# Attention with cluster routing, then a gated feed-forward layer: one more head loaded in half rows, and four pieces of work put elsewhere in the queues

## The chip, the cores and the metric

The kernel runs on one core of a Trainium2 chip. The metric is the device time of one execution in microseconds (us); the kernel before takes 328.75 us in the median of six runs (328.22 to 329.19). A trace of one execution shows for every engine what it ran and when. The engines are named as in the profile: PE (TensorE, matrix products), PEld (its weight loads), DVE (VectorE), ACT (ScalarE), POOL (GpSimd) and SP (SyncE, which here only issues transfers). Times such as "at 79.19" are microseconds from the start of the profiled span.

## What is computed

```python
# q, k, v: (4 batches, 8 heads, 768 tokens, 64); centroids: (8 heads, 16 clusters, 64)
q_assign = argmax(normalised q @ normalised centroids.T)      # one of 16 clusters for each query
k_assign = argmax(normalised k @ normalised centroids.T)      # and for each key
scores = where(q_assign == k_assign, q @ k.T / 8, -1e9)       # (768, 768) for each head
x = softmax(scores) @ v, the heads laid side by side          # (3072, 512)
xn = x / rms(x) * rms_g
out = (silu(xn @ w_gate) * (xn @ w_val)) @ w_out              # 512 -> 1536 -> 512, float32
```

The kernel does without a mask. It adds 16 rows to the 64 rows of each head's transposed q and k: a one-hot code of the cluster, scaled. Where two clusters agree, their product adds a constant to the score, which the exponential takes off again.

## The kernel before

**Names and layout.** The 32 (batch, head) pairs are numbered n = 0 to 31, here called heads. Four heads make a group g (8 groups; groups 2 and 3, heads 8 to 15, are the second batch). Half a batch's queries are a unit u (8 units; u = 2 and 3 are the two halves of batch 1, which is made of groups 2 and 3). A unit is 24 steps, three for each of 8 heads, each with two score products (`s`) and an exponential on ACT (`pT`), followed a head later by the product with v (`acc`).

**How a head gets ready.** Its q and k come from memory into `staged` by SP (`load`). Up to head BH - 1 they are loaded whole, one transfer each for q and k (line 88), then transposed on PE into a PSUM tile `tq` (line 221, three products each for q and for k) and copied to `qkT` by ACT (line 227). From head BH on, each of q and k is loaded in four transfers that put 32-element half rows on different partitions (line 96, eight transfers a head), so that DVE can do the whole transposition in blocks of 32 by 32 (line 217) and neither PE nor ACT has a part in it. POOL casts `qkT` to bfloat16 in `qext` and `kext` (line 240); below BH two of the key casts are DVE's. The cluster steps of a group (`cluster_steps`) are: `products` (PE, line 254, tile `sc`, then a DVE transposition), `most`, `same` and `back` (DVE, lines 262, 266, 286), once for queries and once for keys; `place` then copies the codes below the heads by small transfers that POOL issues (line 297). POOL also casts v (`vcast`, line 243) and issues the weight loads, which convert to bfloat16 on the way; `load_o` (line 207) brings a third of the output weights `wo`.

**The feed-forward part.** When a unit's attention is done, `rms` makes `xn` on DVE (line 403) and SP issues a transposing transfer to `xnT` (line 406). Products `gate` and `val` (line 444) follow, 24 per unit, then 9 pieces of output products `o` (line 469). `gate`, `val`, `o`, `tq` and `sc` take turns on three PSUM tiles (`gen`); ACT and DVE turn `gate` and `val` into `gvT` (lines 452, 453 and 457).

**What sets the order.** The order is written out by hand; every engine and every queue runs its part of it in order. While unit u's attention runs, a list `fill` is worked off between the steps: the last 8 `gate`/`val` products of unit u - 2, `rms` of unit u - 1, late loads, the output products of unit u - 2 with the first rows of preparation for group u + 2 between them (`spread`), and 16 `gate`/`val` products of unit u - 1 with the rest of the preparation. In unit 1 the preparation is that of groups 2 and 3 at once: `prep` is the casts `c`, the cluster steps `a`, and a weave of group 3's transpositions `t3` and casts `c3`. A head's loads for later heads are issued in the middle of its own preparation (`others`: v of head n + 4, q and k of head n + 6), except for the heads in `LATE`, which are issued right behind `rms`, and so behind the transposing transfer on SP's queue.

```python
            if n < BH:      # whole rows: PE transposes later
                (on or nc.sync).dma_start(out=staged[n][:, part], in_=src((q, k)[part], n))
            for e in range(2):      # half rows: four transfers for q, four for k
                for c in range(2):
                    nc.sync.dma_start(out=to[r:r + 32], in_=of[e, c])
```

Of the kernel before, what the change touches and what calls it, by code (L numbers as in the profile page):

```python
# [22 lines left out]
def kernel(  # L23
# [12 lines left out]
    nc = tc.nc  # L36
    B, H, S, D = q.shape
# [7 lines left out]
    HG = 4  # L45
# [4 lines left out]
    FC = DF // P  # L50
# [3 lines left out]
    CUT = 2 * FC - 8  # L54
    LEAD = 6
    NQ, NV = 6, 8
    AV = 4
    LATE = [19] + [n for n in range(20, B * H) if n % HG < 2]
    BH = 14
    BG = BH // HG  # L60

    ctx.enter_context(tc.manual_schedule())
# [17 lines left out]
    def src(a, n):  # L80
        b, h = divmod(n, H)
        return a[b, h].rearrange("(p t) d -> p t d", t=ST)

    def load(n, part, on=None):
        if n not in staged:
            staged[n] = stage.tile([P, 2, ST, D], F32, tag="qk", name="qk")
        if n < BH:
            (on or nc.sync).dma_start(out=staged[n][:, part], in_=src((q, k)[part], n))
            return

        to = staged[n][:, part].rearrange("p t d -> p (t d)").rearrange("p (i r d) -> p i r d", i=HT, d=32)
        of = (q, k)[part][n // H, n % H].rearrange("(r p i e) (c d) -> e c p i r d", p=32, i=HT, e=2, d=32)
        for e in range(2):
            for c in range(2):
                r = 32 * (2 * e + c)
                nc.sync.dma_start(out=to[r:r + 32], in_=of[e, c])

    def load_qk(n):
        if n < B * H:
            load(n, 0)  # L100
            load(n, 1)

    def load_v(n, vq=None):
        if n >= B * H:
            return
        stagedv[n] = stage.tile([P, ST, D], F32, tag="vs", name="vs", bufs=NV)
        (vq or nc.sync).dma_start(out=stagedv[n], in_=src(v, n))
# [98 lines left out]
    def load_o(c):  # L206
        nc.gpsimd.dma_start(out=wo[:, c:c + 4], in_=moe_w_out[c * P:(c + 4) * P].rearrange("(c p) f -> p c f", p=P))
# [4 lines left out]
    def trans(g, h, part, on=None):  # L212
        if (g, h // 2) not in qkT:
            qkT[g, h // 2] = qk32.tile([P, 2, 2, UQ], F32, tag="qkT", name="qkT")
        qk = staged[g * HG + h]
        if g * HG + h >= BH:
            nc.vector.transpose(qkT[g, h // 2][:, h % 2, part], qk[:, part].rearrange("p t d -> p (t d)"))  # L217
            return
        ps = ps_g.tile([P, UQ], F32, tag="gen", name="tq")
        for i in range(HT):  # L220
            nc.tensor.transpose(ps[:, i * P:(i + 1) * P], qk[:, part, 2 * i:2 * i + 2].rearrange("p t d -> p (t d)"),  # L221
                                ident_f)
        to, by = qkT[g, h // 2][:, h % 2, part], 1.0 / ZS if part and g < BG else 1.0
        if on is nc.vector:
            nc.vector.tensor_scalar_mul(to, ps, by)  # L225
        else:
            nc.scalar.activation(to, ps, ACT.Copy, scale=by)
# [5 lines left out]
    def cast(on, g, h, part, es=(0, 1)):  # L233
        for e in es:
            to = cols((kext if part else qext)[g % 4][:D, h], g, e)
            of = qkT[g, h // 2][e * D:(e + 1) * D, h % 2, part]
            if on is nc.scalar:
                nc.scalar.copy(to, of)
            else:
                on.tensor_copy(to, of)  # L240

    def vcast(n):
        nc.gpsimd.tensor_copy(vbf[n // HG % 4][:, n % HG, :, :D], stagedv[n])
# [24 lines left out]
    def cluster_steps(g, m):  # L268

        of = {}  # L270

        def products():
            of["cl"] = cluster_products(g, [(h, m) for h in range(HG)])

        def most():
            of["mx"] = largest(of["cl"])

        def same():
            of["ohT"] = asg.tile([P, UQ], BF16, tag="ohT", name="ohT", bufs=2)
            compare(of["ohT"].rearrange("p (b e c) -> p b e c", e=2, c=NC), of["cl"], of["mx"])  # L280

        def back():
            put[g, m] = asg.tile([P, UQ], BF16, tag="oh", name="oh", bufs=3)
            if m and g >= BG:
                nc.vector.tensor_scalar_mul(of["ohT"], of["ohT"], ZS)
            nc.vector.transpose(put[g, m], of["ohT"])  # L286

        return [products, most, same, back]
# [3 lines left out]
    def place(on, g, m, es=(0, 1)):  # L292

        ext = (kext if m else qext)[g % 4]
        for h in range(HG):
            for e in es:
                on.dma_start(out=ext[D:D + NC, h, e * UQ:(e + 1) * UQ],  # L297
                             in_=put[g, m][32 * h + e * NC:32 * h + (e + 1) * NC])
# [190 lines left out]
    def group_work(g):  # L489

        t, c = [], []
        for h in range(HG):
            n = g * HG + h
            w = 0.0 if n >= BH else 0.3
            t += [(w, lambda h=h: trans(g, h, 0)), (w, lambda h=h: trans(g, h, 1))]

            def others(n=n):
                vcast(n)
                load_v(n + AV)
                if n + NQ not in LATE:  # L500
                    load_qk(n + NQ)

            def both(h=h, f=others):
                cast(nc.gpsimd, g, h, 0)
                f()
                cast(nc.gpsimd if g * HG + h >= BH else nc.vector, g, h, 1, (0,))
            if g == 2:
                c.append((0.0, others))
            else:
                c += [(0.0, both), (0.0, lambda h=h: cast(nc.gpsimd if g * HG + h >= BH else nc.vector, g, h, 1, (1,)))]  # L510
        a = []
        for m in range(2):
            a += [(0.0 if i else 0.7, f) for i, f in enumerate(cluster_steps(g, m))]
            if g == 3:
                a.append((0.0, lambda m=m: place(nc.gpsimd, g, m)))
            elif g == 2:
                a.append((0.0, (lambda: (place(nc.gpsimd, g, 1), place(nc.gpsimd, g, 0, (1,)))) if m else
                          (lambda: place(nc.gpsimd, g, 0, (0,)))))
        if g > 3:
            a[:1] = [(1.4, lambda f=(a[0][1], a.pop(4)[1]): [x() for x in f])]  # L520
            a.append((0.0, lambda: [place(nc.gpsimd, g, m) for m in range(2)]))
        return t, c, a

    def weave(t, c):

        return [x for pair in zip(t, c) for x in pair] + c[len(t):]
# [8 lines left out]
    def spread(a, b):  # L535

        if not a:
            return list(b)
        w, n = [], 0
        for i, x in enumerate(a):  # L540
            w.append(x)
            while n < len(b) * (i + 1) // len(a):
                w.append(b[n])
                n += 1
        return w
# [134 lines left out]
    for u in range(1, NU):  # L680
        ffn, o, g = ffn_work(u - 1), out_work(u - 2) if u > 1 else [], u + 2
        if u == 1:
            t, c, a = group_work(2)
            t3, c3, a3 = group_work(3)
            n = LEAD - 4
            o3 = [(0.0, lambda i=i: load_o(i)) for i in range(0, FC, 4)]
            prep = c + a + spread(weave(t3[n:], c3), o3) + a3[:5]
            idle = const.tile([P, 1], BF16)

            def norm():  # L690
                rms(0)
                nc.gpsimd.tensor_copy(idle, xn[0][:, CC - 1, HT - 1, P - 1:])
                for h in range(HG):
                    casts(pool_, H + h, K0, Q0, K1, Q1)

            hooks = {(1, 0, 0): late[6], (1, 0, 1): lambda: (late[7](), norm())}
            hooks.update({(1, *divmod(2 + i, HT)): t3[i][1] for i in range(n)})
            hooks[1, *divmod(LEAD - 1, HT)] = lambda: xtrans_all(0)
            fill = spread(ffn[:CUT], prep)
            attention([(1, h) for h in range(H)], fill, LEAD, hooks)  # L700
        else:
            fill = ffn_work(u - 2)[CUT:]
            if u == 2:
                fill = fill[:1] + spread(fill[1:], [(0.0, f) for _, f in a3[5:]])
            fill.append((0.0, lambda u=u: rms(u - 1)))
            rows, clusters = group(g)
            fill += [(0.0, lambda n=n: load_qk(n)) for n in LATE if n - n % HG == (u + 3) * HG or (u, n) == (2, 19)]
            n = 12 if u == 2 else len(rows)
            fill += spread(o, rows[:n]) + spread(ffn[:CUT], [(0.0, f) for _, f in rows[n:]] + clusters)
            attention([(u, h) for h in range(H)], fill, 1 if g < NG else 0, ahead=1)  # L710
    rest = ffn_work(NU - 2)[CUT:]
    rest[0][1]()
# [39 lines left out]
```

## Time and profile before

| | |
|---|---|
| median of 6 runs | 328.75 us (328.22 to 329.19) |
| the profiled execution, and its span | 328.22 us, 326.4 us |
| busy: PE, DVE, ACT, POOL | 319.3, 222.4, 246.1, 137.5 us |
| one score product, one gate product, in the table of groups | 327 ns, 325 ns |
| one DVE transposition of half a head, line 217 | 549 ns |
| one ACT copy of half a head, line 227 | 497 ns |
| one cast on POOL, line 240 | 541 to 557 ns |
| granted PE clock | 1.00 in each stretch asked for |

The busy time of an engine is the time in which it had an instruction. Products on PE overlap: each of the products above has a busy time of some 325 ns, but a set of four starts 0.65 us ahead of what follows it. What an instruction costs on a full PE is therefore read from one start to the next. A row in a timeline gives start, duration of the merged run, engine, line, operation, what it writes and reads, and how many. SP's rows are issues of transfers: their duration is the time for which the queue was held, and not the transfer itself.

### The profile page before, as it was taken

Reading aid. Unit: us, or ns where it says so; the run is one execution under the profiler, and the core shown is the slowest. Engines: PE = TensorE matmul, PEld = TensorE weight load, DVE = VectorE, ACT = ScalarE, POOL = GpSimd, SP = SyncE. Lnnn points to the kernel's source line nnn. Section 1 sums busy time; section 2 is a strip of 40 time slices with the busy share of each in tenths; the row PEclk is TensorE's granted clock in tenths of the full one; section 3 lists DMA queues with packets and bytes.
Section 4 is the critical chain, followed back from the end, with each engine's and each line's share of the span. In section 5 each row is a group of like instructions: output and inputs, shape, how many; then the busy total and the mean of one; then the engine's idle time right before and its main releaser. Section 6 shows DMA issues by size and latency. Waiting matters only on the chain.

```text
span 326.4 us, 7794 instructions
## 1 busy us (share of the span) xinstructions
PE 319.3 (98%) x2851; PEld 192.0 (59%) x2865; DVE 222.4 (68%) x509; ACT 246.1 (75%) x425; POOL 137.5 (42%) x277
## 2 busy tenths in 40 slices
PE   8999899999999999999999999999999999999996
PEld 4546656655556655665566555665566656655654
DVE  5999978879478676878677785876265645685430
ACT  5899988977769867897778867897779868862322
POOL 6999499995926265441916256350000000000000
PEclk9999999999999999999999999999999999999999
DMA  7999995798546654561545540000700041002002
GB/s 274 373 259 209 230 166 101 126 193 167 95 65 145 142 114 74 120 157 52 100 87 120 154 112 34 8 20 1 148 2 0 2 112 34 0 2 79 20 1 96
DMA packets 88742, 34.24 MB, mean 105 GB/s; under 512 B 70400, under 2 KB 85632, under 8 KB 88704
## 3 DMA queue, kind: packets, MB, share of 16 engines
q1 hardware_dynamic: 79536, 27.45, 35.5%
q0 software_dynamic: 8880, 5.91, 11.1%
q8 instruction: 22, 0.36, 0.5%
q10 hardware_dynamic: 288, 0.39, 0.3%
q14 instruction: 16, 0.13, 0.1%
HBM read 28.61 MB, written 6.29 MB: 107 GB/s over the span
## 4 chain that ended last, share of the span: by engine, by line
PE 87%; DVE 9%; ACT 2%; issue 1%; POOL 0%; DVEq 0%; ACTq 0%; POOLq 0%
PE gate L444 18%; PE val L444 18%; PE o L469 18%; PE s L348 17%; PE acc L366 9%; PE sc L254 3%; ACT pT L352 1%; DVE kext L332 1%; DVE qext L332 1%; PE warm L132 1%; DVE pads L327 1%; PE tq L221 1%; PE o L480 1%; DVE qkT L225 1%; DVE xn L391 1%
## 5 line engine op out<-in xcount | busy, mean ns | idle before, releaser
L352 ACT ACTIVATE pT<-s,off 128x768 bf16<-128x768 f32 x192 | 170.9, 904 | 30.9 <-PE s L348 30.2
L348 PE MATMUL s<-qext,kext 80*128 80x384 bf16 x384 | 94.8, 327 | 1.6 <-ACT pT L352 0.8
L444 PE MATMUL gate<-xnT,wg 128*128 128x384 bf16 x384 | 78.3, 325 | 0.1
L444 PE MATMUL val<-xnT,wv 128*128 128x384 bf16 x384 | 78.1, 326 | 0.0
L453 DVE SCALAR_TENSOR_TENSOR th<-th,gate 128x384 f32<-128x384 f32 x84 | 46.3, 551 | 34.8 <-ACT th L452 34.2
L469 PE MATMUL o<-wo,gvT 128*128 128x512 bf16 x262 | 66.3, 378 | 0.8
L348 PEld LDWEIGHTS <-kext 80*128 80x128 bf16 x384 | 36.4, 98 | 35.1 <-issue 7.5
L452 ACT ACTIVATE th<-gate 128x384 f32<-128x384 f32 x84 | 41.2, 490 | 15.3 <-PE gate L444 14.5
L457 DVE SCALAR_TENSOR_TENSOR gvT<-th,val 128x384 bf16<-128x384 f32 x84 | 46.2, 550 | 9.3 <-PE val L444 3.4
L444 PEld LDWEIGHTS <-wg 128*128 128x128 bf16 x384 | 36.1, 97 | 23.4 <-issue 0.8
L366 PEld LDWEIGHTS <-pT 128*128 128x128 bf16 x1152 | 43.4, 97 | 10.1 <-DVE x L373 1.0
L444 PEld LDWEIGHTS <-wv 128*128 128x128 bf16 x384 | 35.6, 97 | 22.5 <-issue 0.6
L240 POOL CAST qext<-qkT 64x384 bf16<-64x384 f32 x64 | 35.3, 557 | 30.7 <-DVE inv L371 18.4
L366 PE MATMUL acc<-vbf,pT 128*128 128x65 bf16 x1152 | 45.7, 193 | 0.6 <-ACT pT L352 0.2
L469 PEld LDWEIGHTS <-gvT 128*128 128x128 bf16 x276 | 25.9, 97 | 25.6
L297 POOL DMA_DIRECT2D qext<-oh x48 | 23.0, 490 | 32.7 <-DVE oh L286 29.2
L240 POOL CAST kext<-qkT 64x384 bf16<-64x384 f32 x58 | 31.4, 541 | 4.3 <-DVE qkT L225 2.4
L297 POOL DMA_DIRECT2D kext<-oh x48 | 23.1, 488 | 7.5 <-DVE oh L286 7.1
L472 ACT COPY o_sb<-o 128x512 f32<-128x512 f32 x23 | 13.5, 585 | 16.0 <-PE o L469 16.0
L371 DVE RECIPROCAL inv<-acc 128x6 f32<-128x6 f32 x32 | 6.0, 188 | 23.8 <-PE acc L366 23.4
L373 DVE TENSOR_TENSOR x<-acc,inv 128x384 f32<-128x384 f32 x32 | 17.8, 558 | 1.1
L217 DVE STREAM_TRANSPOSE qkT<-qk 128x384 f32<-128x384 f32 x36 | 18.1, 549 | 0.0
(83 smaller groups left out, 230.1 us busy)
## 6 DMA issues: line engine op xcount, KB each, us to landing
vs<-in_v_dram SPq DMA_DIRECT2D x32, 192.0 KB, 4.2
out_dram<-o_sb SPq DMA_DIRECT2D x23, 256.0 KB, 2.7
qk<-in_q_dram SPq DMA_DIRECT2D x72, 48.0 KB, 2.8
qk<-in_k_dram SPq DMA_DIRECT2D x72, 48.0 KB, 2.6
qk<-in_q_dram SPq DMA_DIRECT2D x14, 192.0 KB, 4.1
qk<-in_k_dram SPq DMA_DIRECT2D x12, 192.0 KB, 4.2
wg<-in_moe_w_gate_dram POOLq DMA_DIRECT2D x4, 384.0 KB, 8.5
wv<-in_moe_w_val_dram POOLq DMA_DIRECT2D x4, 384.0 KB, 9.7
```

Source lines behind the costliest of these rows:

```text
L217: nc.vector.transpose(qkT[g, h // 2][:, h % 2, part], qk[:, part].rearrange("p t d -> p (t d)"))
L240: on.tensor_copy(to, of)
L297: on.dma_start(out=ext[D:D + NC, h, e * UQ:(e + 1) * UQ], in_=put[g, m][32 * h + e * NC:32 * h + (e + 1) * NC])
L348: nc.tensor.matmul(ps[:, j, :w] if nt == HT else flat[:, j * w:(j + 1) * w], lhsT=cols(kext[g % 4][:KR, hh], g, kc // HT, kc % HT * P, (kc ...
L352: nc.scalar.activation(pT[u, h][:, n * i:n * i + n, :w], of, ACT.Exp, bias=off, scale=scale if g >= BG else scale * ZS)
L366: nc.tensor.matmul(acc[:, h % 2, t], lhsT=pT[u, h][:, kc, t * P:(t + 1) * P], rhs=vbf[g % 4][:, hh, kc % HT * 2 + kc // HT], start=kc == 0 ...
L373: nc.vector.tensor_tensor(dst, acc[:, :, :nt, :D], inv[:, :, :nt].unsqueeze(3).broadcast_to([P, 2, nt, D]), op=ALU.mult)
L444: nc.tensor.matmul(ps, lhsT=w[:, c, f * P:(f + 1) * P], rhs=xnT[u][:, c, :n], start=c == 0, stop=c == CC - 1)
L452: nc.scalar.activation(th, ps, ACT.Tanh, scale=0.5)
L453: nc.vector.scalar_tensor_tensor(th, th, 1.0, ps, op0=ALU.add, op1=ALU.mult)
L457: nc.vector.scalar_tensor_tensor(gvT[u][:, f, :n], gates[u], 0.5, ps, op0=ALU.mult, op1=ALU.mult)
L469: nc.tensor.matmul(outs[u], lhsT=gvT[u][:, f, t * P:(t + 1) * P], rhs=wo[:, f], start=f == 0, stop=f == FC - 1)
```

## The change

- BH goes from 14 to 13: head 13 is loaded in half rows and transposed on DVE.
- `LATE` becomes a table by unit. Head 18's q and k are no longer loaded from the middle of head 12's preparation in unit 1, but with 19, 20 and 21 behind unit 2's `rms(1)`; heads 24, 25, 28 and 29 stay where they were.
- The first two `load_o` go from the weave of group 3 into group 2's cluster steps, between the placing of the key codes and that of the second half of the query codes. The third goes into the weave behind its fourth entry.
- In unit 2, 8 and no longer 12 of group 4's 16 rows go between the output products; the other 8 (heads 18 and 19) and the first four cluster steps go among the 16 `gate`/`val` products. The key's `most`, `same` and `back`, and the placing, go to unit 3, among its first `gate`/`val` products.

```diff
-    LATE = [19] + [n for n in range(20, B * H) if n % HG < 2]
-    BH = 14
+    LATE = {2: (18, 19, 20, 21), 3: (24, 25), 4: (28, 29)}
+    BH = 13
...
-                if n + NQ not in LATE:
+                if not any(n + NQ in x for x in LATE.values()):
                     load_qk(n + NQ)
...
             elif g == 2:
-                a.append((0.0, (lambda: (place(nc.gpsimd, g, 1), place(nc.gpsimd, g, 0, (1,)))) if m else
-                          (lambda: place(nc.gpsimd, g, 0, (0,)))))
+                a += [(0.0, lambda: place(nc.gpsimd, g, 1)), (0.0, lambda: load_o(0)), (0.0, lambda: load_o(4)),
+                      (0.0, lambda: place(nc.gpsimd, g, 0, (1,)))] if m else [(0.0, lambda: place(nc.gpsimd, g, 0, (0,)))]
...
-            o3 = [(0.0, lambda i=i: load_o(i)) for i in range(0, FC, 4)]
-            prep = c + a + spread(weave(t3[n:], c3), o3) + a3[:5]
+            w3 = weave(t3[n:], c3)
+            prep = c + a + w3[:4] + [(0.0, lambda: load_o(8))] + w3[4:] + a3[:5]
...
-            if u == 2:
-                fill = fill[:1] + spread(fill[1:], [(0.0, f) for _, f in a3[5:]])
+            if u in (2, 3):
+                fill = fill[:1] + spread(fill[1:], [(0.0, f) for _, f in (a3[5:] if u == 2 else rest)])
             fill.append((0.0, lambda u=u: rms(u - 1)))
             rows, clusters = group(g)
-            fill += [(0.0, lambda n=n: load_qk(n)) for n in LATE if n - n % HG == (u + 3) * HG or (u, n) == (2, 19)]
-            n = 12 if u == 2 else len(rows)
-            fill += spread(o, rows[:n]) + spread(ffn[:CUT], [(0.0, f) for _, f in rows[n:]] + clusters)
+            fill += [(0.0, lambda n=n: load_qk(n)) for n in LATE.get(u, ())]
+            n, m = (8, 4) if u == 2 else (len(rows), len(clusters))
+            fill += spread(o, rows[:n]) + spread(ffn[:CUT], [(0.0, f) for _, f in rows[n:]] + clusters[:m])
+            rest = clusters[m:]
```

## The prediction

> **What bounds the kernel now.** I read the page's busy times and its chain first, then PE's timeline around head 13, then SP's queue across units 1 to 3, and the stretches of four microseconds last.
>
> ```profile
> PE 319.3 (98%) x2851; PEld 192.0 (59%) x2865; DVE 222.4 (68%) x509; ACT 246.1 (75%) x425; POOL 137.5 (42%) x277
> PE 87%; DVE 9%; ACT 2%; issue 1%; POOL 0%; DVEq 0%; ACTq 0%; POOLq 0%
> ```
>
> PE is hardly ever without work from 41 us on, and the chain that ended last runs along it. So a microsecond taken from PE's list is a microsecond of the kernel, unless another queue then makes PE wait. Here is head 13, which the change takes off PE:
>
> ```profile
> 51.81 0.51 PE L348 MATMUL s<-qext,kext 80*128 80x384 bf16 x2
> 52.15 0.49 PE L221 MATMUL tq<-ident_f,qk 128*128 128x128 f32 x3
> 52.48 0.81 PE L444 MATMUL val<-xnT,wv 128*128 128x384 bf16 x4
> 53.13 0.51 PE L348 MATMUL s<-qext,kext 80*128 80x384 bf16 x2
> 53.72 0.55 PE L221 MATMUL tq<-ident_f,qk 128*128 128x128 f32 x3
> 54.10 0.81 PE L444 MATMUL gate<-xnT,wg 128*128 128x384 bf16 x4
> 53.72 0.31 PEld L221 LDWEIGHTS tq<-ident_f,qk 128*128 128x128 f32 x3 [0.49 <-ACT qkT L227]
> ```
>
> The reader is to see starts, not durations: the first `tq` pushes its follower from 52.15 to 52.48, the second costs 0.38 and had a hole in front of it, because its PSUM tile came free late. SP's queue is the second thing that has no room:
>
> ```profile
> 71.94 1.81 SPq L107 DMA_DIRECT2D vs<-in_v_dram  x3
> 79.19 1.63 SPq L406 DMA_TRANSPOSE xnT<-xn  x1
> 80.87 2.95 SPq L96 DMA_DIRECT2D qk<-in_q_dram  x4
> 83.87 2.63 SPq L96 DMA_DIRECT2D qk<-in_k_dram  x4
> ...
> 109.45 2.63 SPq L96 DMA_DIRECT2D qk<-in_k_dram  x4
> 112.18 0.56 SPq L473 DMA_DIRECT2D out_dram<-o_sb  x1
> 112.84 0.86 SPq L107 DMA_DIRECT2D vs<-in_v_dram  x2
> 116.45 1.49 SPq L406 DMA_TRANSPOSE xnT<-xn  x1
> ```
>
> From 80.87 to 113.70 SP issues without a pause: five heads in half rows (19 to 23), outputs and v. Then it waits 2.75 us, until `xn` of unit 2 is ready. The transposing transfer at 116.45 took 3.8 us to land, so `xnT` is there at 120.25. Its first reader on PE starts at 123.09:
>
> ```profile
> 122.55 0.71 PE L366 MATMUL acc<-vbf,pT 128*128 128x65 bf16 x18
> 123.09 0.81 PE L444 MATMUL gate<-xnT,wg 128*128 128x384 bf16 x4
> ```
>
> **The change, part by part.**
>
> *Head 13 off PE and ACT.* Two sets of three transpositions. First set: 52.48 - 52.15 = 0.33. Second: the `s` before it needs 0.33 from 53.13, so PE was free at 53.46; `gate` started at 54.10; 0.64 with the hole. Together 0.97 us. The lower end is without the hole, 0.33 + 0.38 = 0.71, if some other tile is late there instead. The hole goes with its cause, though: the tile that the second `tq` takes is the one of `gate` at 51.16, whose DVE reader ran from 53.15 to 53.67; without the two `tq` the third tile back is always one whose reader has been done for 0.9 us or more, by the same timeline. I take 0.97. Here a rule is weighed: the Trainium skill, "TensorE: Matmul & The Clock Gate", section "PE-mode transpose", measures about 275 ns for one 128x128 transposition inside a kernel; six would be 1.65 us (an estimate from that page, for another type). The busy times of the trace (0.49 for three that start 0.11 apart) show why that is too much: they overlap their neighbours. The spacing decides, 0.97. ACT loses two copies of 0.49, which lie beside PE.
>
> *Head 13 on DVE and POOL.* DVE gains two transpositions at 0.55 and gives two key casts at 0.39 to POOL: net +0.3 us between 52 and 62 us. DVE idled there for 0.46 + 0.35 us, and again 0.76 ahead of 63.25, and its work for head 13 begins at 54.24, as before. Laying the new order on these starts, `gvT` follows its `val` by 2.0 to 2.2 us where it was 1.8 to 2.1, and three PSUM tiles leave 0.9 us. Cost nothing; were that cover gone, PE would pay the 0.3. POOL gains two casts, 1.0 us, while group 3's codes are placed at 81.4 and wanted near 93.
>
> *Head 13's loads.* Two whole transfers held SP for 0.80 us (28.75 to 29.55); eight in half rows hold it 5.3 us where nothing else is on (2.63 for four), and 10.6 us (32.80 to 43.43, head 14) in the crowded stretch. Queued behind them are v of heads 8 to 12, then heads 14 and 15. The stretch is full until 46 us and half empty behind (last two figures of a row: share of the transfer engines' time, summed over packets so that it can pass 1, and GB/s):
>
> ```profile
> 40.00:44.00 4.00, 3.73 (x41) 2.30 (x41) 2.46 (x7) 3.50 (x6) 3.20 (x8) 1.00 1.54 213
> 48.00:52.00 4.00, 4.00 (x44) 2.10 (x42) 3.10 (x7) 3.08 (x4) 3.90 (x10) 1.00 0.50 79
> 57.24 0.56 DVE L217 STREAM_TRANSPOSE qkT<-qk 128x384 f32<-128x384 f32 x1
> 60.82 0.57 DVE L217 STREAM_TRANSPOSE qkT<-qk 128x384 f32<-128x384 f32 x1
> ```
>
> Everything behind is 4 to 6 us later. Heads 14 and 15 (the last two lines: their key transpositions) then land at 52 to 54 and 56 to 59 in place of 47.6 and 53; they are wanted at about 57 and 60. v of 8 to 11 lands by 46 and POOL takes it at 49.16. Nothing waits if the delay stays under 6 us. I cost it at zero; at 8 us PE would pay about 1.5.
>
> *Head 18 behind the transposing transfer.* Unit 1's queue loses 7.6 us (64.30 to 71.94) and is early again, but the transfer at 79.19 waited for `xn`, not for SP: no gain. In unit 2 the queue gains eight issues. What was head 19's slot (80.87) now holds 18; DVE wants 18 where it wanted 19 (88.44), and that one didn't wait. Head 19 lands at about 93 less 1.0 and is wanted a few tenths later: zero. The outputs behind are 5.3 us later, with three buffers that are not needed before 113. But the queue's end moves. PE and `xn` come 0.97 earlier, so: 79.19 - 0.97 = 78.22 for unit 1's transposing transfer; the old stretch from there to the end of v, 113.70 - 79.19 = 34.51; one head more, 2.63 x 2 and gaps, 5.3; end 118.0. The next transposing transfer goes out at 118.0 where `xn` is ready at 116.45 - 0.97 = 115.5. It lands 3.8 later, up to 4.7 as the one at 79.19 did beside other traffic (two v transfers are in flight now): 121.8 to 122.7. `gate` wants it at 123.09 - 0.97 = 122.1. Wait: nothing to 0.6 us; near the shorter landing, which four of the six such transfers have, 0.15. I take 0.15. A rule speaks against the half rows: the Trainium skill, "DMA: Bandwidth & Descriptors", section "Bandwidth", gives 0.95 us for a 64 KB transfer and calls those under 64 KB descriptor-dominated. Eight at 0.95 would be 7.6 us (an estimate from that page, for another issuer); SP would end 2.3 us later, PE wait about 2.4, and the change lose 1.4. The trace has 0.62 to 0.66 for one of these 48 KB transfers in unit 2, so 5.3 stands.
>
> *`load_o` earlier.* Same three issues of 0.76 to 0.79 on POOL. The third was issued at 69.34 and its median landing is 7.2, so 76.5, and `o` reads it at 76.82 without a wait. Now there is slack; it was no loss. What is moved behind the first two (the query's second half) is not read before unit 3. POOL's wait of 3.58 us at 73.47 for a full queue may go, in cover.
>
> *Cluster steps.* Unit 2's product `sc` changes its place, not its cost. The key's three steps and a scaling (0.55 + 0.55 + 0.25 + 0.58 = 1.9 us of DVE) leave unit 2, which gets two more transpositions (1.1), and enter unit 3's first eight products, where DVE idled 2.7 us between 103.99 and 112.45. Group 3's same steps lie there in unit 2 (69 to 75 us) without a hole on PE. Placing ends near 114 or somewhat later and is read in unit 4: zero.
>
> Sum: -0.97 + 0.15 = -0.8 us. The profiled execution goes from 328.22 to 327.4 (span 325.6). It lies 0.53 below the median, so the median goes from 328.75 to 327.95, say 328.0.
>
> **Rivals.**
>
> *The transposing transfer takes most of it back* (unit 3 waits 0.35 to 1.6 us). For it: the end of SP's queue, 118.0, is a sum over 48 issues, and a few in the trace took 0.9 longer than the rest; landing 4.7 was seen twice. Against: 3.8 is commoner. Time 328.1 to 329.4, centre 328.6.
>
> *Slower: the same transfer, but with SP's pieces slower.* In the stretch 64.30 to 71.84 eight issues took 7.5 us, 0.94 each. If unit 2's 48 pieces ran at 0.70 in place of 0.65, the queue would end 2.4 us later and PE wait 2.5: net +1.6, 330.3. It decides against the change once PE waits more than 0.97 + 0.66 = 1.63, which is an issue at about 119.5 or later: 0.03 us on each piece. Against: no weights load in that stretch now.
>
> *Loads in unit 1 too late* (heads 14, 15 above): net about +0.5 at a delay of 8 us, 329.3. Against: the stretch behind 46 us is half empty.
>
> *The change doesn't do what it says:* DVE stalls where PE had worked, and the gain is only the 0.71, or nothing. 328.0 to 328.75.
>
> **How the numbers follow.** 0.2% is 0.66 us, about what a measurement of this kernel can tell. Full gain with a wait below 0.35: 0.46, range 327.6 to 328.1. Most of it given back: 0.28. Slower by slow pieces: 0.14. Late loads in unit 1: 0.04. Gain absent by DVE: 0.08. Faster than 328.09 is the first case nearly whole and a sliver of the others, 0.46; slower than 329.41 takes the third, most of the fourth when it is large, and some of the second's tail, 0.19; the rest 0.35. The range runs from 327.4 (0.97 down, and the 0.4 or so that single runs of before lie off their median) to 329.5, which leaves out the slow-piece case and little else.
>
> **What would show it.** The two `tq` sets of head 13 gone and `val` straight behind `s` near 52.15; DVE's transpositions of heads 13 to 15 without a wait for a transfer; SP's second transposing transfer issued right behind v, near 118.0, and landing near 122; the first `gate` of unit 3 near 122.2; units 4 to 7 unchanged in length. It is wrong if `gate` in unit 3 waits over 0.35 us, if SP ends unit 2 later than 118.5, or if DVE waits for heads 14, 15, 18 or 19.

## The result, and the profile after

The changed kernel takes 329.62 us in the median of 19 executions (328.0 to 332.81), the kernel before beside it 328.68 us (40 executions): 1.0049 of the time before, with a 95% interval of 1.0032 to 1.0066. Here it is slower, by half a per cent. On a later occasion the same two kernels gave 328.81 and 328.69 us, a ratio of 1.0006 (0.9993 to 1.002): no gain there either. The prediction was 328.0.

The profiled execution of after is its longest, 332.81 us with a span of 331.0, where before had 328.22 and 326.4. First its page: the head, busy times, the shares of the chain that ended last, and the group of the `gate` products with the idle time in front of it.

```profile
span 331.0 us, 7790 instructions
PE 319.4 (96%) x2845; PEld 191.3 (58%) x2859; DVE 222.5 (67%) x509; ACT 245.1 (74%) x423; POOL 139.0 (42%) x279
PE 81%; DVE 9%; DMA 4%; ACT 2%; issue 1%; SPq 1%; DVEq 0%; ACTq 0%
L444 PE MATMUL gate<-xnT,wg 128*128 128x384 bf16 x384 | 79.0, 327 | 3.3 <-DMA xnT<-xn 3.2
```

PE is as busy as before, though it has six products fewer: part of its work ran at a lower clock. The chain has lost 6 points of PE, and 4 points of DMA are new in it. The group names the place: one wait of 3.2 us for `xnT`. The chain in order of time shows what stands ahead of it (start, duration, engine or transfer):

```profile
115.21 2.30 DMA qk<-in_k_dram
118.29 7.33 DMA xnT<-xn
125.66 1.44 PE gate L444 x4
```

SP's queue of after, and PE behind it (start, duration of the run, engine, line, operation, count, and the wait in brackets):

```profile
113.87 2.63 SPq L96 DMA_DIRECT2D qk<-in_k_dram  x4
116.59 0.56 SPq L473 DMA_DIRECT2D out_dram<-o_sb  x1
117.25 0.87 SPq L107 DMA_DIRECT2D vs<-in_v_dram  x2
118.29 1.32 SPq L406 DMA_TRANSPOSE xnT<-xn  x1
119.67 5.50 SPq L96 DMA_DIRECT2D qk<-in_q_dram  x4
...
121.74 0.71 PE L366 MATMUL acc<-vbf,pT 128*128 128x65 bf16 x18
125.66 1.44 PE L444 MATMUL gate<-xnT,wg 128*128 128x384 bf16 x4 [3.21 <-DMA xnT<-xn]
126.89 1.48 PE L444 MATMUL val<-xnT,wv 128*128 128x384 bf16 x4
```

The transposing transfer of unit 3 goes out right behind v, as forecast, and lands 7.33 us later instead of 3.8. Then four `gate` products take 1.44 us where four took 0.81 before. The stretches of one microsecond say why (stretch, length, busy time and count of PE, PEld, DVE, ACT and POOL, granted PE clock, share of the transfer engines' time, GB/s):

```profile
122.00:123.00 1.00, 0.45 (x15) 0.36 (x12) 0.48 (x2) 1.00 (x2) 0.57 (x2) 1.00 0.06 9
123.00:124.00 1.00, 0.00 (x0) 0.00 (x0) 0.28 (x1) 0.00 (x1) 0.30 (x1) 1.00 0.18 43
124.00:125.00 1.00, 0.00 (x0) 0.00 (x0) 0.00 (x0) 0.00 (x0) 0.94 (x3) 1.00 1.29 273
125.00:126.00 1.00, 0.34 (x2) 0.17 (x2) 0.00 (x0) 0.00 (x0) 0.90 (x3) 0.58 0.64 99
126.00:127.00 1.00, 1.00 (x5) 0.48 (x4) 0.00 (x0) 0.00 (x0) 0.94 (x3) 0.50 0.60 94
128.00:129.00 1.00, 1.00 (x8) 0.30 (x10) 0.77 (x2) 0.10 (x1) 0.00 (x0) 0.71 0.46 74
```

The clock is granted in full while PE is idle, falls to half just as PE resumes, and is back at about 128.6. From 122 to 124 the transfer engines moved almost nothing, 9 and 43 GB/s: the transfer was not crowded out, it had stalled, and so had the four issues behind it (5.50 us for four, 3.69 before). One thing stands next to the stall in the trace: a block of program. From 118.29 to 125.61 the queue for instructions, q8, moved one packet of 0.02 MB (16 KB), at 121.24; the second line is the transposing transfer with its time to landing:

```profile
q8 instruction: 1, 0.02, 0.8%
xnT<-xn SPq DMA_TRANSPOSE x1, 7.3
```

What such a block has to do with a late landing is taken up below, with all profiles.

Where the 4.6 us of span went can be laid out completely. The start runs to unit 1's first `gate`, unit 1 from there to the first `o` of unit 2, units 2 and 3 from one unit's first `o` to the next one's, and the tail from the first product of the last output piece (line 480) to the end of the span. A span is given to a tenth, so a tail is good to 0.05.

| us | start | unit 1 | unit 2 | unit 3 | the rest | tail | span |
|---|---|---|---|---|---|---|---|
| before | 41.23 | 32.52 | 37.30 | 37.17 | 172.57 | 5.61 | 326.4 |
| after | 41.52 | 31.56 | 37.17 | 41.95 | 172.57 | 6.23 | 331.0 |
| after, second profile | 41.35 | 31.57 | 37.16 | 38.09 | 172.58 | 6.25 | 327.0 |

Three things stand out. Unit 1 is 0.96 shorter, unit 2 0.13. Unit 3 is 4.78 longer: 3.2 of wait, the rest mostly the half clock. And 0.62 us that nobody looked for lies in the tail.

The executions of after fall in two groups: of 20 on record, 13 took 328.0 to 330.15 with a mean clock of 0.998 to 1.000, and seven 331.2 to 332.81 with 0.993 to 0.995, the profiled one among them; on the later occasion three of 21 took 331.31 to 333.27. The second profile is of an execution of the shorter group; that run comes first below.

### The profile page after: what moved, and what is told of

Same layout as the page of the kernel before. It is cut to its first block, busy times and chain, and to the rows that moved or that the text cites. A ratio compares the mean times of both kernels' runs of the same rounds, so it can differ in the third digit from the quotient of the medians.

```text
span 331.0 us, 7790 instructions
## 1 busy us (share of the span) xinstructions
PE 319.4 (96%) x2845; PEld 191.3 (58%) x2859; DVE 222.5 (67%) x509; ACT 245.1 (74%) x423; POOL 139.0 (42%) x279
## 4 chain that ended last, share of the span: by engine, by line
PE 81%; DVE 9%; DMA 4%; ACT 2%; issue 1%; SPq 1%; DVEq 0%; ACTq 0%
PE gate L444 18%; PE val L444 18%; PE s L348 16%; PE o L469 15%; PE acc L366 9%; PE sc L254 3%; DMA xnT<-xn 2%; DVE kext L332 1%; DVE qext L332 1%; DVE pads L327 1%; SPq L96 1%; DMA boot<-in_centroids_dram 1%; ACT pT L352 1%; PE o L480 1%; DVE qkT L225 1%
## 5 line engine op out<-in xcount | busy, mean ns | idle before, releaser
L240 POOL CAST kext<-qkT 64x384 bf16<-64x384 f32 x60 | 32.6, 544 | 4.7 <-DVE qkT L225 2.7
L217 DVE STREAM_TRANSPOSE qkT<-qk 128x384 f32<-128x384 f32 x38 | 19.3, 550 | 0.0
```

## The experiments

Some of the expectations name other runs: e2 is before with head 13 alone, e4 is after with v issued behind the transposing transfer, e8 is after with head 24 ahead, e10 is before with v last.

**Is the landing of 7.3 us the order's, or one execution's?** The kernel after, unchanged.

> The kernel after unchanged, profiled a second time. If the 7.3 us that unit 3's transposing transfer took to land belongs to the order of the queue, it is over 6 again and the first gate of unit 3 waits over 2 us; if 7.3 is the long end of a spread that this order has (5.0 to 5.4 with neighbouring orders), it is 4.5 to 6 and the gate waits 0.3 to 2. Median 329.6 either way.

Measured: 328.81 us (before 328.69), and in its profile:

```profile
117.94 1.32 SPq L406 DMA_TRANSPOSE xnT<-xn  x1
119.31 3.10 SPq L96 DMA_DIRECT2D qk<-in_q_dram  x4
...
123.05 0.81 PE L444 MATMUL gate<-xnT,wg 128*128 128x384 bf16 x4 [0.76 <-DMA xnT<-xn]
```

Issue to first reader is 5.1 us, the wait 0.76, and the clock stays up. The expected median was missed, but the landing is as the second of the two readings had it: 7.3 is the long end of a spread, and 5.1 is still above the 3.8 to 4.7 of before. With it unit 3 is 0.92 longer and the tail 0.64; with the start's 0.12 that takes back more than the 0.96 and 0.13 of units 1 and 2. That sum is +0.6 us in the span (327.0 against 326.4), without any loss of clock.

**Which part brings what?** The kernel before with `BH = 13` alone:

```diff
-    BH = 14
+    BH = 13
```

> The kernel before with head 13 in half rows and nothing else of the change. Theory (SP's queue): unit 2's queue is as before, so unit 3's first gate does not wait; unit 1's queue is 4 to 5 us longer and ends near 78, just where the transposing transfer of unit 2 is due, so between 327.7 us and, if that one is late, 329. Rival (half rows cost by themselves): slower than before, 329.5 or more, without a wait for xnT in unit 3.

Measured: 332.28 us, 1.0112 (1.0079 to 1.0145). Unit 1 is 31.57, so head 13's gain is there in full. Unit 2 is 38.94, and this is why:

```profile
71.06 0.74 POOL L207 DMA_DIRECT2D wo<-in_moe_w_out_dram  x1
77.88 1.02 PE L469 MATMUL o<-wo,gvT 128*128 128x512 bf16 x4 [1.62 <-DMA wo<-in_moe_w_out_dram]
```

The last third of `wo` is issued 1.7 us later than the 69.34 of before, and PE is earlier. The profiled execution was the shortest of its kind (329.89), so 1.6 is probably the small end of this wait. The transposing transfer of unit 2, behind it, took 6.50 us to land, and nothing waited for it. The other way round, after with all but head 13:

```diff
-    BH = 13
+    BH = 14
```

> The changed kernel with head 13 in whole rows again, through PE: the other three parts of the change alone. Theory (SP's queue): no 0.97 us is won, and SP's queue is as full in unit 2 as in the changed kernel; the transposing transfer goes out near 119 and lands 4 to 7 us later, unit 3's first gate waits 0.5 to 3 us and the clock may drop behind it: 329.5 to 331.5, not faster than the changed kernel. Rival (head 13's half rows are the cost): 328.7, as before.

Measured: 329.5 us, 1.0032 (1.0017 to 1.0046). Unit 1 has its old 32.49, the tail its old 5.66; unit 3 is 37.69, with the same wait as in after:

```profile
117.83 2.18 SPq L406 DMA_TRANSPOSE xnT<-xn  x1
123.09 0.81 PE L444 MATMUL gate<-xnT,wg 128*128 128x384 bf16 x4 [0.37 <-DMA xnT<-xn]
```

So the wait in unit 3 does not need head 13, and the longer tail does come with it. The profiled execution is again near the shortest (328.39 of 328.33 to 332.54); that the usual wait is longer than 0.37 is likely, but not shown. Third, after with head 18 loaded in unit 1 again:

```diff
-    LATE = {2: (18, 19, 20, 21), 3: (24, 25), 4: (28, 29)}
+    LATE = {2: (19, 20, 21), 3: (24, 25), 4: (28, 29)}
```

> The changed kernel, but with head 18's q and k loaded in unit 1 again, as before; all else as changed. Theory (SP's queue): the transposing transfer of unit 3 goes out when xn is ready, near 115.5, lands 3.8 to 4.5 us later and the first gate of unit 3 does not wait; PE keeps the 0.97 us of head 13 and the clock stays at 1.00: 327.7 us, ratio 0.997. Rival (the half rows of head 13 or the moved cluster steps themselves cost the time): the median stays near that of the changed kernel, 329.6.

Measured: 328.24 us beside 328.46, 0.9992 (0.9979 to 1.0006). SP issues unit 3's transposing transfer at 116.34, and nothing waits for it. The wait of 0.44 us is now in unit 2, whose transposing transfer goes out at 80.76 in place of 78.54, behind head 18's eight. Moving head 18 moves the late transfer from one unit to the next.

**Is it the issue behind v that costs?** After, with v of heads 22 and 23 issued behind unit 3's transposing transfer:

```diff
-                load_v(n + AV)
+                if n + AV not in (22, 23):
+                    load_v(n + AV)
...
+            fill += [(0.0, lambda n=n: load_v(n)) for n in ((22, 23) if u == 3 else ())]
```

> The changed kernel with the loads of v for heads 22 and 23 issued behind unit 3's transposing transfer and not ahead of it; everything else as changed. If the landing of 7.3 us (3.8 before) comes from the two v transfers in flight ahead of it: issue near 117.3, landing 3.8 to 4.5, at 121.1 to 121.8, and no wait at the gate: 327.7 to 328.0. If it comes from the traffic of the half rows, or from being issued behind any busy queue: landing 5 to 7 us again, a wait of 1 to 2.5 us, 329 or more.

Measured: 327.95 us beside 328.46, 0.9985 (0.9976 to 0.9994): faster than before. SP and PE:

```profile
116.70 0.56 SPq L473 DMA_DIRECT2D out_dram<-o_sb  x1
117.43 1.63 SPq L406 DMA_TRANSPOSE xnT<-xn  x1
119.16 1.85 SPq L107 DMA_DIRECT2D vs<-in_v_dram  x2
...
122.47 0.81 PE L444 MATMUL gate<-xnT,wg 128*128 128x384 bf16 x4
```

The transfer goes out 0.86 earlier than in after and lands 5.00 later, at 122.43; PE's wait is gone but for hundredths (unit 3 is 37.24, where 37.17 is the shortest). The loss in unit 3 is shown to lie in this one transfer, issued 0.9 us too late. Why it takes 5 us is another question: v no longer stands ahead of it, and the landing is as long as in the second profile of after, so v in flight is not what lengthens it. The same kernel with the four q transfers of head 18 left in unit 1 as well:

> As e4 (v of heads 22 and 23 behind unit 3's transposing transfer), and head 18's q alone loaded in unit 1 again, ahead of the last three v; its k stays in unit 2. Theory (the end of SP's queue decides): SP's idle 3.7 us at the end of unit 1 takes the four issues, unit 2's queue ends 2.6 us earlier, at about 114.8, so that the transfer goes out when xn is ready, near 115.6, and never waits for SP; no run pays for a late landing: 327.3 to 327.7, ratio to before 0.997. Rival (what is left of the gain is lost elsewhere, not in the landing): 327.9 as e4.

Measured: 327.94 us, 0.9984 (0.9968 to 1.0). The landing is 3.7 here, and nothing is gained by it: once the transfer is in time, more room is worth nothing.

Does v itself, or whole-row transfers in general, delay a transposing transfer behind them? The kernel before, with the four q transfers of head 24 and v of 22 and 23 put directly ahead of it, in two orders (v last, or the half rows last):

```diff
+            if u == 3:
+                fill += [(0.0, lambda: load(24, 0)), (0.0, lambda: load_v(22)), (0.0, lambda: load_v(23))]
...
+            if u == 3:
+                fill.append((0.0, lambda: load(24, 0)))
```

> The kernel before, with head 24's q (four half-row transfers) and behind them v of heads 22 and 23 ahead of unit 3's transposing transfer; SP then has no pause ahead of it, and the issue stays near 116.4. If whole transfers in flight ahead of it slow the landing: 5 us or more, in place of 3.8. No wait at the gate unless the landing passes 6.6 us: 328.5 to 329.

> As e10 with the order turned round: v of heads 22 and 23 first, then head 24's q in four half-row transfers, then the transposing transfer. If it is whole transfers in flight that slow the landing: 3.8 to 4.3 us here, less than in e10. If any busy queue does it: the same as in e10, 5 us or more. Time 328.5 to 329.

Measured: 328.9 us (1.0009) and 328.51 us (1.0006), both intervals reach below 1. The transfer goes out at 116.84 and 117.05 and lands in 4.2 and 4.3 us. The order of the two kinds makes no difference, and neither brings a landing above 5. All profiles side by side show more (landing of unit 3's transposing transfer, and how long SP had issued nothing ahead of it):

| SP's pause ahead of it | kernels | landing |
|---|---|---|
| 1.0 us or more | before; 13 alone; 18 early; v behind with q of 18 early; v behind with `load_o` back; before with six and with eight more transfers (below) | 3.7 to 4.0 |
| 0.34 and 0.16 us, four half rows and v ahead | the two above | 4.2, 4.3 |
| 0.16 to 0.18 us, eight half rows and an output ahead | after twice; all but 13; v behind; steps back; v behind with two, three (twice) and eight more transfers (below) | 5.0 to 5.6, and once 7.3 |

Within unit 3 the pause looks like the mark of a short landing, with two exceptions: in the two kernels below with 16 half rows of head 24 ahead, the queue is unbroken (0.17 us) and the landing is 3.8. But the other units break the rule. Unit 6's transposing transfer goes out behind a pause of 31 us in every profile, and in 17 of 20 it takes 4.8 to 5.4 us, in the kernel before 4.89 (at 228.54). What fits much better is the block of program of the section on the result. There are 22 or 23 such blocks of 16 KB in a run. Over the six transposing transfers of each of the 20 profiles:

| start of a 16 KB block on q8 | transfers | landing |
|---|---|---|
| none between issue and landing, units 3 to 7 | 65 | 3.66 to 3.83 |
| none between issue and landing, unit 2 | 18 | 3.84 to 4.96 |
| 0.5 us behind the issue | 1 | 4.17 |
| 1.4 to 3.0 us behind the issue | 15 | 4.83 to 7.33 |
| 3.1 to 3.7 us behind the issue | 21 | 3.76 to 5.65 |

All 23 landings of more than 4.97 us have a block in them. The two exceptions have none, and unit 6's transfers have one. From unit 6 of before, and from unit 3 of the kernel with head 24 ahead, whose transfer queues from issue to landing have no q8:

```profile
q8 instruction: 1, 0.02, 1.2%
xnT<-xn SPq DMA_TRANSPOSE x1, 4.9
...
q1 hardware_dynamic: 2728, 0.54, 78.8%
xnT<-xn SPq DMA_TRANSPOSE x1, 3.8
```

In before, unit 3's transfer was just ahead of a block: that starts 3.12 us behind the issue, and the landing is 3.76. In after it starts 2.95 and 1.59 us behind the issue (7.33 and 5.07). This is a correlation over 120 transfers. No run moves a block and nothing else, so that the block is the cause is likely and not shown; why one that starts 3.1 to 3.7 us behind the issue costs 1.6 us in some profiles and nothing in others, and why once 7.3, is open.

**What did the parts costed at zero do?** The kernel with v behind, but with the three `load_o` back in the weave of group 3:

```diff
+            o3 = [(0.0, lambda i=i: load_o(i)) for i in range(0, FC, 4)]
+            prep = c + a + spread(weave(t3[n:], c3), o3) + a3[:5]
```

> As e4, but with the three issues of the output weights back in the weave of group 3, as in the kernel before. By the prediction's step (the earlier issue only adds slack to a load that was not late): 327.9 as e4. Rival (eight more half-row transfers ahead of them make the output weights late, as a wait of 1.6 us for wo in e2 suggests): unit 2's output products wait 1 to 4 us for wo, 329 to 332.

Measured: 332.46 us, 1.0098 (1.0069 to 1.0127); the kernel with q of 18 early, beside it on the same chip, took 327.94. In its profile, another 2.69 us in unit 2:

```profile
70.40 0.74 POOL L207 DMA_DIRECT2D wo<-in_moe_w_out_dram  x1
78.30 1.02 PE L469 MATMUL o<-wo,gvT 128*128 128x512 bf16 x4 [2.69 <-DMA wo<-in_moe_w_out_dram]
```

And with all the cluster steps left in unit 2:

```diff
-            n, m = (8, 4) if u == 2 else (len(rows), len(clusters))
+            n, m = (8, len(clusters)) if u == 2 else (len(rows), len(clusters))
```

> As e4, but with all cluster steps of group 4 in unit 2 again (heads 18 and 19 still prepared among the gate and val products). By the prediction (moving them costs and brings nothing): 327.9 as e4, unit 2 and unit 3 of the same length as there. Rival (DVE gets too full in unit 2 with two more transpositions and the steps): unit 2 longer by 0.3 to 1 us, 328.3 to 329.

Measured: 329.03 us beside 328.82, 1.0004 (0.9992 to 1.0016). Unit 2 is 38.22 in place of 37.17. DVE waits 1.52 us for the key of head 19, and PE behind DVE:

```profile
93.27 0.58 DVE L217 STREAM_TRANSPOSE qkT<-qk 128x384 f32<-128x384 f32 x1 [1.52 <-DMA qk<-in_k_dram]
94.35 1.51 PE L254 MATMUL sc<-qkT,cblk 128*32 128x384 f32 x16 [0.97 <-DVE th L453]
```

Neither move takes work off PE. They are what lets head 13 and head 18 move: without the one the kernel loses 4.5 us in the median, without the other 1.1.

**How does the loss of clock grow with the wait?** After, with head 24's loads put ahead of unit 3's transposing transfer. The edit put more there than it meant to: head 24 is loaded twice, so 16 transfers came ahead and not eight.

```diff
-    LATE = {2: (18, 19, 20, 21), 3: (24, 25), 4: (28, 29)}
+    LATE = {2: (18, 19, 20, 21), 3: (25,), 4: (28, 29)}
...
+            if u == 3:
+                fill.append((0.0, lambda: load_qk(24)))
```

> The changed kernel with head 24's eight transfers ahead of unit 3's transposing transfer instead of behind it: the suspected wait made longer on purpose. Theory: issue 5.3 us later, near 123.6, landing 4 to 7 us later; the gate of unit 3 waits 5.5 to 8.5 us, and PE's granted clock falls to half for 2 to 3 us behind the wait (1.2 to 1.6 us more): 335 to 338. Rival (the loss in the changed kernel is not this wait): no more than 331.

The second kernel adds 20 products of 512 columns on PE, whose result nobody reads, ahead of unit 3's first `gate`:

```diff
+            ... spread(o, rows[:n]) + ([(0.0, lambda: busy(20, False))] if u == 3 else []) + ...
```

> As e8, with 20 products without use (4.3 us of PE) put ahead of unit 3's first gate, so that PE is idle there for under 3 us; the useful work is the same. Theory (part of the loss is the lower clock behind a long idle time): the gate starts at the same time as in e8, no lower clock behind it, 1.2 to 1.6 us faster than e8. Rival (the clock has no part, or the lower clock comes from the wait itself): as e8, or slower.

Measured: 340.05 us (1.0356) and 341.25 us (1.0388). Of the first, PE and three stretches:

```profile
132.80 1.44 PE L444 MATMUL gate<-xnT,wg 128*128 128x384 bf16 x4 [10.69 <-DMA xnT<-xn]
...
126.00:127.00 1.00, 0.00 (x0) 0.00 (x0) 0.00 (x0) 0.00 (x0) 0.94 (x3) 0.86 0.45 70
127.00:128.00 1.00, 0.00 (x0) 0.00 (x0) 0.00 (x0) 0.00 (x0) 0.39 (x1) 0.50 0.56 88
136.00:137.00 1.00, 1.00 (x9) 0.40 (x12) 0.11 (x1) 0.81 (x1) 0.00 (x0) 0.52 0.33 56
```

The wait was 10.69 and 7.42 us, longer than either expectation, and the 20 products (122.4 to 126.9) did not bridge it: PE was idle for 7.4 us behind them. So filling the hole was not put to the test. What the two do show: the time lost beyond wait and filler is the same for both waits. Against the kernel with v behind, from the first `gate` to the last output piece, they have 12.75 - 10.69 = 2.1 us and 14.0 - 7.42 - 4.48 = 2.1 us; after has 4.70 - 3.21 = 1.5, its second profile 0.85 - 0.76 = 0.1. It is about half of the time that PE then worked at half clock: 4.2, 4.5 and 2.9 us.

**What is the 0.6 us in the tail?** With v behind no unit has a wait, and from the first `gate` to the last output piece it takes 278.55 us where before takes 279.56: 1.0 less. The median is only 0.5 lower. The tail is 6.21 to 6.28 us in all seven kernels so far that have the change's six additional transfers (eight half rows for two whole ones) and no further ones, and 5.61 to 5.69 in the four with head 13 whole. PE's work in it is the same. In the built program SP's transfers take eight completion counters in turn; six more put the last three outputs on the third to fifth counter, where before had them on the fifth to seventh. If the closing sequence on SP goes over the counters in order, it has more left to do behind the last landing. This can be tried with small transfers alone: the one load of the norm's weights near the start is cut into pieces, here into four (three more transfers), with v behind:

```diff
-    nc.sync.dma_start(out=grow, in_=moe_rms_g.unsqueeze(0).broadcast_to([P, DM]))
+    gs = [DM * i // 4 for i in range(5)]
+    for a, b in zip(gs, gs[1:]):
+        nc.sync.dma_start(out=grow[:, a:b], in_=moe_rms_g[a:b].unsqueeze(0).broadcast_to([P, b - a]))
```

> The kernel after with v of heads 22 and 23 behind unit 3's transposing transfer, and the one small load of the norm's weights near the start cut into three pieces, so that SP issues two more transfers. The units should be as long as without the cut (31.56, 37.17, 37.2 us for units 1 to 3). Theory of the tail: SP's transfers take eight completion counters in turn; head 13's six more transfers moved the last three outputs from the fifth to seventh counter to the third to fifth, and the closing sequence, which goes over the counters in order, has more left to do after the last landing. Two more transfers bring them back to the fifth to seventh: from the last output projection's first product to the end of the span 5.6 us in place of 6.2, and about 327.4 us in the median (0.9963 of before). Rival, that the tail belongs to head 13's work or to the clock: 6.2 us stays, about 328.0.

> The kernel before, with the same small load cut into seven pieces: six more transfers on SP, as many as the change adds, and none of its other parts. Theory of the tail: 6.2 us from the last output projection's first product to the end in place of 5.6, units unchanged, median 0.6 us above before (1.0018). Rival, that the tail belongs to head 13's work: 5.6 us and the time of before.

> As the kernel with two more transfers, but three: the last outputs take the last three counters. Theory of the tail: one step of the closing sequence fewer, 5.3 to 5.6 us, about 327.2 in the median. Rival: 6.2 us and 328.0.

Two more gave a tail of 6.04 and not 5.6, so the turn of the counters alone doesn't explain it. Another thing moves with the number of transfers: SP's program grows, and a block of program (8 KB, on the queue for instructions) is fetched 1.3 us behind the end of the span in before, but 0.2 to 0.3 ahead of it where the tail was 6.0 to 6.2. Eight more transfers keep the counters and move the code:

> As the kernel with two more transfers, but eight: the last three outputs are on the third to fifth completion counter again, as in the kernel after, and SP's program is longer than in any run so far. Theory of the counters: 6.2 us from the last output projection's first product to the end, about 328.0 in the median. Theory of the code load: what lengthens the tail is an 8 KB block of program fetched between the last landing and the end; it came 0.3 to 0.4 us ahead of the end where the tail is 6.2 and 6.0, and earlier than the last landing where three more transfers gave 5.55. With eight more it is fetched earlier still: 5.5 to 5.6 us, about 327.4.

> The kernel before with the small load in nine pieces: eight more transfers, so every transfer behind takes the counter that it takes in the kernel before. Theory of the counters: tail 5.6 us, median as before. Theory of the code load: the block is fetched between the last landing and the end as in the other kernel that has eight more than before (6.0 us there): 6.0 us, and 0.3 to 0.4 above before.

| kernel | transfers more than before | tail | median (before beside it) | ratio |
|---|---|---|---|---|
| before | 0 | 5.61 | | |
| before, six more | 6 | 6.24 | 329.34 (328.69) | 1.0014 (1.0003 to 1.0026) |
| before, eight more | 8 | 5.65 | 328.78 (328.19) | 1.0017 (1.0006 to 1.0028) |
| v behind | 6 | 6.23 | 327.95 (328.46) | 0.9985 (0.9976 to 0.9994) |
| v behind, two more | 8 | 6.04 | 327.82 (328.69) | 0.9973 (0.9964 to 0.9981) |
| v behind, three more | 9 | 5.55 | 327.29 (328.69) | 0.9957 (0.9945 to 0.9969) |
| v behind, eight more | 14 | 5.81 | 328.06 (328.19) | 0.9995 (0.9984 to 1.0005) |

Six more transfers bring the long tail into the kernel before without any work of head 13: the tail belongs to the number of transfers, and that is shown. How is not. By the counters the two kernels with eight more than before should both have 5.6, and that with 14 should have 6.2: two rows miss. The two expectations from the code load missed as well (5.5 to 5.6 and 6.0), but they had taken the time of the fetch for granted. By the time at which the block really comes, all rows fit: 0.2 to 0.3 us ahead of the end with every tail of 6.0 to 6.2, and with the short ones 0.6 ahead (nine more; before with eight), 1.1 to 1.2 (14 more) or behind the end. No run moves that block alone, so this is not shown. The two kernels with head 24 twice also have 14 more: one has 5.82, the other, with the 20 products, 6.4. In that one the last output landed 5.3 us behind the first product of line 480 and not 4.7, with a 16 KB block starting 2.8 us behind it; from the last landing to the end both have 1.1. Nor does the tail alone make the medians: before with eight more has the short tail and is still 0.6 us slower. In the profile of before with six more, `wo` came 0.61 us late in unit 2; the one with eight has no such wait, and what its median lost is open.

Is three more a gain or chance? Its 327.29 rested on five executions, so it was run again, unchanged:

> The kernel with v of heads 22 and 23 behind unit 3's transposing transfer and three more small transfers, unchanged, measured and profiled again. If its 327.29 us is its own, the median is 327.2 to 327.6 (0.995 to 0.997 of before), with 5.5 to 5.6 us from the last output projection's first product to the end. If it was a lucky set of few executions, the median is near the 327.9 of the kernel without the three transfers, and the tail 5.8 to 6.2.

Measured: 327.37 us beside 328.47, 0.9971 (0.9959 to 0.9983), with this end:

```profile
319.59 2.81 PE L480 MATMUL o<-wo,gvT 128*128 128x256 bf16 x36
core 0: 325.2 us, clock 1.000
```

The tail is 325.2 - 319.59 = 5.61. The gain is real, about 1.1 to 1.4 us, and this version (the change, v of 22 and 23 behind unit 3's transposing transfer, three more small transfers) beats both kernels.

## Why the prediction was wrong

**Right: head 13 off PE.** It forecast 0.97 from starts. Unit 1 is 0.96 shorter in every profile with head 13 in half rows and `load_o` early, and `val` stands behind `s` as forecast:

```profile
52.09 0.51 PE L348 MATMUL s<-qext,kext 80*128 80x384 bf16 x2
52.44 0.81 PE L444 MATMUL val<-xnT,wv 128*128 128x384 bf16 x4
53.09 0.51 PE L348 MATMUL s<-qext,kext 80*128 80x384 bf16 x2
```

The loads in unit 1 came in time, too: DVE waits for none of heads 13 to 15. Weighing the spacing against the price of a single transposition was the right choice.

**Right: when SP gets there.** 118.0 forecast, 118.29 and 117.94 measured; the sum over 48 issues held to 0.3 us. The rival of slower pieces did not occur.

**Wrong: "it lands 3.8 later, up to 4.7".** This is the step that failed. It measured 5.1 and 7.3. The 3.8 was that of a transfer issued at 116.45, with a block of program starting 3.12 us behind it. Going out 1.5 to 1.8 us later, it had the block 1.59 to 2.95 us behind its issue, where none of 15 transfers landed in under 4.8. Nor was 4.7 an upper end in the trace that the prediction had: of the two landings that it calls 4.7 one is 4.66, the other, at 228.54, is 4.89, and SP had issued nothing for 31 us ahead of that one. What is shown is the landing of 5.1 and 7.3 and that this transfer made PE wait; that the block made it long is the likely cause. With 5.1 on 118.0 the first `gate` would have been forecast at 123.1, a wait of 1.0 in place of 0.15, and the gain would have been all but gone: the case listed as the first rival, with 0.28. The second profile is that case (wait 0.76, range of the rival 0.35 to 1.6).

**Missing: the price behind a wait.** A wait was costed at its own length. One of 3.2 us cost 4.7, because PE's clock was at half for the first 2.9 us of its work afterwards (half of that is 1.5). The prediction's slower rival, too, should have carried this.

**Missing: the tail.** Six transfers more were costed at the time for which they hold the queue, near the start, and not at the other end of the program, where 0.6 us hangs on their number. The forecast -0.8 would have been -0.2 with this alone.

**Wrong in meaning: two zeros.** "Now there is slack; it was no loss" holds for the profiled execution of before, in which `wo` was just in time. In the variant of before with v last it was 0.46 us late, with six more transfers 0.61, with head 13 in half rows 1.62 and 2.69. The move is what pays for head 13's loads. So too the cluster steps: "head 19 is wanted a few tenths later" is true because they moved; unmoved, they cost 1.05. Neither error is in the sum, since the change has both moves.

The range ended at 329.5; the first measurement is 0.1 above it, the second inside. The chance for faster, 0.46, leaned on the landing time.

## What to carry to other kernels

A transfer's time to landing in one profile is no upper bound for the same transfer issued at another time, even where a queue was idle ahead of it: here the long landings go with a block of program that is fetched meanwhile. The transfer that PE waits for is put ahead of what can come later (here two loads of v, worth the difference between 1.0049 or 1.0006 and 0.9985). A wait of a few microseconds on PE costs more than its length. A load that is just in time in one profile is not slack, and a change in the number of transfers is to be looked for at the end of the program too.

## What the runs showed of the hardware

- The clock of PE fell to half 2.7 us after PE went idle in after, 4.6 us and 5.2 us after in the two kernels with head 24 ahead, and not at all in idle times of 0.76, 1.62 and 2.69. It came back 2.9, 4.2 and 4.5 us after PE resumed. The Trainium skill, "TensorE: Matmul & The Clock Gate", section "What's actually happening", states one free-running window of about 3.4 us for both ways. Times that vary fit a free-running window; the 2.7 and the 2.9 are shorter than one whole window of that length.
- Transposing transfers landed in 3.7 to 3.8 us where no 16 KB block of program was fetched between issue and landing (65 in units 3 to 7; 3.8 to 5.0 in unit 2), and in 4.8 to 7.3 where one started 1.4 to 3.0 us behind the issue (15 transfers). In the case of 7.3 the transfer engines moved 9 and 43 GB/s for two microseconds while it was on its way.
- The time from the first product of the last output piece to the end of the span was 5.55 to 6.28 us for the same work on PE, by the number of transfers that SP issued earlier, and 6.4 in the kernel with the 20 products.
